# Loading q and k of five early tiles in 2-KB pieces and turning them with 64-column products

## The chip, the cores and the metric

The kernel runs on one core of one Trainium2 chip. The metric is the device time of one execution in microseconds (us); of three timed runs of the kernel before, the median is 197.52 us (197.02 to 198.58). Engines are named as in the profile: PE is the matrix engine (PEld its weight loads), DVE the vector engine, ACT the scalar engine, POOL the engine whose queue issues the loads from memory, SP the engine whose queue issues the stores and the transposing DMAs.

## The reference

Two stages follow each other. The first is attention with 4 batches, 8 heads, 768 positions and head size 64. Position i sees the 8 first positions and the 96 last ones up to its own; the score carries a slope per head times the distance. The result, written as 3072 tokens of 512 numbers, goes through a two-layer network: `relu(x @ w_in) ** 2 @ w_out` with `w_in` 512 x 2048 and `w_out` 2048 x 512.

```python
scores = scale * np.matmul(q, k.transpose(0, 1, 3, 2))
scores = np.where(keep, scores + bias, -1e9)      # keep: first 8 keys, or 0 <= i - j < 96
a = np.exp(scores - scores.max(-1)); a = a / a.sum(-1)
x = np.matmul(a, v)                               # -> (3072, 512)
out = np.maximum(x @ w_in, 0.0) ** 2 @ w_out
```

## The kernel before, in words

The 3072 tokens are 24 tiles j of 128 positions (six per batch); two tiles make a block of 256 tokens for the network, so there are 12 blocks. For a tile the chain is: load q and k (type changed to bfloat16 on the way), turn them so that the head dimension lies on the partitions (`tr.0.j` for q, `tr.1.j` for k on PE into a PSUM bank, `T.0.j` and `T.1.j` copy the bank to `qkT` on ACT or DVE), bias products (`bias`, tiles 0 to 2 only), score products (`sc`), exponentials on ACT (`exp`), a multiplication by a mask on DVE (`mul`, from tile 3 on), the products with v (`pv`), a division on DVE (`norm`), turning the result (`trx` on PE and `xT` as its copy, tiles 0 to 7). `gk` and `gv` copy the 8 global keys and values from the batch's first tile into the next ones. From tile 8 on q and k are turned by transposing DMAs.

The network's first layer is `s1.block.step` in plain form (block 0 and half of block 1), and later `h.block.group.product` with seven products for eight (Strassen's scheme), with sums of the weights (`isum`, `wsum`), copies `u`, additions `c` and squares `q`. The second layer is `s2.block.product` with `part` copies, `o` results and `st` stores.

The order of all this is written out by hand in `ORDER` (line 57 on). It is a list of names; each engine runs its own names in the order of the list, one after the other, and waits in front of each one for whatever that needs. `@A` and `@V` put a copy on ACT or DVE, the hex digits behind a colon pick PSUM banks or buffers. So an engine never runs a later name while an earlier one waits. The SBUF pieces `qk_first` hold q and k of tiles 0 to 5; later the same memory takes `isum`.

Tile 0 comes through SP in float32 (`plain`). Tiles 1 to 5 are loaded by `load_part` on POOL: every row of 64 numbers of a head is one 256-byte piece, 1024 pieces for 128 positions and 8 heads. The issuing line in the profile is L330. `emit_tr` (L528) turns a tile with four 128x128 transposes, one for each pair of heads, and `emit_T` (L455 on DVE, L453 on ACT) copies the bank, which holds bfloat16. In `ORDER` fourteen loads stand before the first load of `w_in`, `ld.win.1.0`, on POOL's queue: the ten loads of q and k and those of v for tiles 0 to 3.

Of the kernel before, what the change touches and what calls it, by code (L numbers as in the profile page):

```python
# [62 lines left out]
trx.1:6 exp.3.0.1 exp.3.1.0:7 exp.3.0.0 ld.win.1.0 pv.2.0:2 pv.2.1:5 norm.2.0:0 norm.2.1 gv.2@V mul.3.0:8 sc.4.0:1037
exp.4.1.0:9 trx.2:2 ld.win.4.0 xT.1@A exp.4.1.1:a tr.1.5:4 tr.0.5:5 T.1.5@A exp.4.0.0 xT.2@A:1 mul.3.1:b pv.3.0:0
pv.3.1:6 T.0.5@A s1.0.1:7 norm.3.0:1 gk.4@V exp.4.0.1 norm.3.1 gv.3@A s1.0.1#2 trx.3:4 sc.5.0:0126 exp.5.0.1:c
exp.5.1.0:d s1.0.4:5 exp.5.1.1 E0.0 mul.4.0:e xT.3@V ld.v.4 mul.4.1:f ones.6 pv.4.0:3 s1.1.1:4 relu.0.4@V:2 exp.5.0.0
ld.win.3.0 s1.0.3:2 pv.4.1:1 relu.0.1@A:0 sq.0.1@A:0 gv.4@A s1.0.3#2 mul.5.1:1 s1.1.3:6 norm.4.0:0 norm.4.1 ld.win.2.0
ld.win.0.0 s1.0.0:5 relu.0.3@A:3 sq.0.3@A mul.5.0:5 gate.10 s1.0.2:0 trx.4:7 relu.1.1@A:4 sq.1.1@A:1 xs.1.0:0 ld.v.5
ld.win.2.1 pv.5.0:3 ld.win.0.1 pv.5.1:1 xs.1.1 ld.win.6.0 ld.win.7.0 ld.win.5.0 relu.1.3@A:7 norm.5.0:1 norm.5.1
ld.wout.3 s1.1.2:2 xT.4@A:2 relu.1.2@A:8 ld.wout.2 ld.wout.1 ld.wout.0 isum.0.0 s1.1.0:4 s1.0.2#2 trx.5:3 gate.14  # L70
xT.5@V relu.1.0@A:6 sq.1.2@A s1.0.0#2 xs.2.0:1 h.2.0.p1:1 sq.1.0@V sq.0.4@A u.2.0.1@A:b isum.3.0 sq.1.3@A xs.2.1
ld.wout.7 isum.0.1 s1.0.0#3 s1.0.6:6 gate.11 isum.1.0 isum.1.1 xs.1.2 s1.0.7:7 h.2.0.p2:2 c.2.0.c11:9 h.2.1.p1:3
relu.0.6@A:a ld.wout.6 ld.wout.5 ld.wout.4 u.2.1.1@A:e relu.0.7@A:c isum.3.1 s1.0.0#4 h.2.1.p5:4 s1.0.2#3 relu.0.0@A:f
h.1.1.p1:6 h.2.1.p2:7 u.1.1.1@A:0 isum.2.1 h.2.1.p6 u.2.1.2@A:d h.1.1.p2:2 c.1.1.c11:3 xs.2.2 c.2.1.c11:5 sq.0.0@A
s1.0.2#4 isum.2.0 h.1.1.p6 u.1.1.2@A:1 h.2.0.p6 u.2.0.2@A:4 h.2.1.p7 u.2.1.3@A:8 h.1.1.p7 h.2.0.p5:5 relu.0.2@A:6
u.1.1.3@A:2 h.2.0.p7 wsum.0.0 h.1.1.p5:2 u.2.0.3@A:7 c.2.1.c22:b wsum.1.0 sq.0.2@A gate.9 s1.0.5:7 h.2.1.p3 wsum.2.0
c.2.0.c22:f load.6 load.7 c.1.1.c22:0 sq.0.7@A relu.0.5@A:e sq.0.6@A sq.0.5@A load.8 c.2.1.c12:8 sum.0.2:0 sum.0.0
h.1.1.p4 h.2.0.p4 wsum.0.1 s2.1.p1.0:0 T.8 c.2.0.c21@A:6 h.2.0.p3 h.2.1.p4 s2.0.p1.0:7 h.1.1.p3 sum.0.1 s2.0.p2.0:4
q.1.1.c22@A q.1.1.c11@A s2.0.p1.1 q.2.1.c22@A:2 q.2.0.c11@A part.0.p1@A:0 c.1.1.c21@A:c s2.0.p2.1 s2.1.p1.1 wsum.1.1
s2.0.p6.0 s2.0.p6.1 c.1.1.c12:7 tr.1.6:1 tr.0.6:6 part.1.p1@A:1 q.1.1.c21@A s2.1.p2.0:2 q.2.1.c11@A sum.0.3 wsum.2.1  # L80
part.0.p6@A:2 o.0.p2:a c.2.1.c21@A:2 s2.1.p2.1 wsum.3.1 wsum.3.0 T.1.6@V s2.0.p7.0 s2.0.p7.1 gate.12 s2.0.p5.0
q.1.1.c12@A s2.0.p5.1 c.2.0.c12:e load.9 part.0.p7@A:3 q.2.1.c12@A T.0.6@A q.2.0.c22@A o.0.p5:d s2.0.p4.0 s2.0.p4.1
q.2.0.c12@A o.0.p4@A sum.1.0:1 s2.0.p3.0 tr.0.7:3 gate.13 sum.1.1 s2.0.p3.1 o.1.p2:0 o.0.p3 sum.1.2 T.0.7@A tr.1.7:1
sum.2.2:0 sum.1.3 sum.2.0 T.1.7@A q.2.0.c21@A s2.1.p6.0 s2.1.p6.1 q.2.1.c21@A part.1.p6@A:0 sc.6.0:567341 exp.6.1.0:3
load.10 gk.7@A exp.6.0.0 s2.1.p5.0 s2.1.p7.0 s2.1.p7.1 mul.6.0:b exp.7.0.0:9 exp.7.1.0 part.1.p7@A:3 s2.2.p1.0:6
s2.1.p5.1 sum.2.1 exp.7.0.1:1 exp.7.1.1 o.1.p5:c mul.7.0:5 s2.2.p1.1 pv.6.0:5 norm.6.0:0 s2.1.p4.0 s2.1.p4.1 o.1.p4@A
pv.6.1:7 s2.1.p3.0 sc.8.0:3415 exp.8.0.1:7 part.2.p1@A:1 pv.7.0:0 s2.1.p3.1 mul.7.1:8 norm.6.1 T.9 pv.7.1:7 norm.7.0:1
norm.7.1 trx.6:1 exp.8.1.0:4 xT.6@V:0 exp.8.1.1 exp.8.0.0 s2.2.p6.0 s2.2.p6.1 o.1.p3 gate.15 trx.7:0 xT.7@A gk.8@V
mul.8.1:f h.3.1.p1:4 u.3.1.1@A:e gv.7@V h.3.0.p2:7 sc.9.0:5132 exp.9.0.1:6 exp.9.1.0:2 xs.3.0:0 xs.3.1 exp.9.0.0
h.3.0.p1:0 h.3.1.p6 mul.8.0:3 s2.2.p2.0:3 u.3.0.1@V:9 pv.8.0:1 u.3.1.2@A:b T.10 c.3.0.c11:1 h.3.0.p6 pv.8.1:5  # L90
norm.8.0:0 exp.9.1.1 sum.2.3 norm.8.1 xs.3.2 part.2.p6@A:2 xT.8:2 s2.2.p2.1 h.3.1.p7 h.3.1.p5:7 u.3.0.2@A:5
u.3.1.3@A:8 c.3.1.c22:7 o.2.p2:4 mul.9.0:3 mul.9.1:9 h.3.0.p7 s2.2.p7.0 s2.2.p7.1 u.3.0.3@A:f q.3.1.c22@A:0
part.2.p7@A:3 q.3.0.c11@A h.3.0.p5:2 h.3.1.p2:1 c.3.1.c11:8 gv.8@V load.11 c.3.0.c22:7 h.3.1.p3 h.3.0.p4 c.3.0.c21@A:2
h.3.1.p4 c.3.1.c21@A:1 q.3.1.c11@A c.3.1.c12:6 s2.2.p5.0 pv.9.0:5 gk.9@V T.11 st.0.0 norm.9.0:1 q.3.1.c12@A
q.3.0.c22@A h.3.0.p3 pv.9.1:1 gv.9@A c.3.0.c12:e norm.9.1 s2.3.p1.0:0 s2.2.p5.1 sc.10.0:4752 exp.10.1.1:f h.4.0.p1:1
s2.2.p4.0 exp.10.1.0:3 s2.2.p4.1 q.3.0.c12@V s2.3.p1.1 sum.3.0:1 o.2.p5:b s2.2.p3.0 s2.2.p3.1 exp.10.0.1 exp.10.0.0
part.3.p1@A:0 sum.3.1 h.4.1.p1:2 s2.3.p6.0 o.2.p4@A mul.10.0:8 s2.3.p6.1 sum.3.2 pv.10.0:7 mul.10.1:9 o.2.p3 gk.10@A
xT.9 norm.10.0:0 xs.4.0:1 xs.4.1 h.4.1.p2:5 pv.10.1:4 q.3.1.c21@A q.3.0.c21@A part.3.p6@A:1 u.4.1.1@A:6 u.4.0.1@A:5
s2.3.p7.0 s2.3.p7.1 h.4.1.p6 u.4.1.2@A:7 norm.10.1 h.4.0.p6 u.4.0.2@A:e gate.18 sc.11.0:6374 exp.11.1.0:a exp.11.0.0
gv.10@V c.4.1.c11:3 part.3.p7@V:3 sum.3.3 xs.4.2 load.12 h.4.0.p2:5 T.12 exp.11.1.1:1 h.4.1.p7 s2.3.p4.0 mul.11.0:2  # L100
exp.11.0.1 c.4.0.c11:f u.4.1.3@A:8 mul.11.1:9 load.13 h.4.0.p7 h.4.1.p5:3 c.4.1.c22:6 s2.3.p2.0:6 pv.11.0:4
u.4.0.3@A:a norm.11.0:1 q.4.1.c11@A:1 h.4.1.p4 h.4.0.p5:7 c.4.0.c22:5 s2.3.p2.1 o.3.p2:2 pv.11.1:5 q.4.1.c22@A
h.4.1.p3 q.4.0.c11@A gate.16 norm.11.1 h.4.0.p4 c.4.1.c21@A:1 c.4.0.c21@A:3 h.4.0.p3 s2.3.p4.1 c.4.1.c12:8 q.4.1.c12@A
c.4.0.c12:6 T.13 s2.3.p5.0 s2.3.p5.1 o.3.p5:9 q.4.0.c22@A q.4.0.c21@A o.3.p4@A sc.12.0:425137 exp.12.0.0:a st.2.1
exp.12.1.0 exp.13.0.0:b exp.13.1.0 exp.13.0.1:f q.4.0.c12@V s2.3.p3.0 sum.4.2:0 sum.4.0 xT.10:1 h.5.1.p1:0 s2.3.p3.1
mul.12.0:7 s2.4.p1.0:4 xT.11 o.3.p3 gate.19 xs.5.0:0 xs.5.1 h.5.0.p1:2 u.5.0.1@A:e q.4.1.c21@A h.5.1.p2:5 s2.4.p1.1
sum.4.1 part.4.p1@A:2 u.5.1.1@A:8 load.15 load.14 st.2.0 st.3.1 h.5.0.p5:1 pv.12.0:6 h.5.0.p6 mul.13.0:5 h.5.0.p2:3
c.5.0.c11:3 norm.12.0:0 s2.4.p6.0 xs.5.2 u.5.0.2@A:6 exp.13.1.1 mul.13.1:a q.5.0.c11@A:2 h.5.1.p6 h.5.0.p7 pv.12.1:7
u.5.0.3@A:4 s2.4.p2.0:3 s2.4.p6.1 s2.4.p2.1 pv.13.0:6 c.5.0.c22:1 gk.13@V h.5.0.p3 u.5.1.2@A:9 c.5.1.c11:b h.5.0.p4
norm.13.0:1 q.5.0.c22@A part.4.p6@A:0 norm.12.1 pv.13.1:5 norm.13.1 o.4.p2:e h.5.1.p7 gate.21 c.5.0.c12:3 h.5.1.p5:6  # L110
s2.4.p7.0 s2.4.p7.1 c.5.0.c21@A:7 q.5.0.c21@A u.5.1.3@A:f load.16 st.1.0 T.14 q.5.1.c11@V c.5.1.c22:0 h.5.1.p4 T.15
sum.4.3 T.16 sc.14.0:7251 xT.12:0 gv.13@A xT.13 q.5.1.c22@V q.5.0.c12@A s2.4.p5.0 part.4.p7@A:3 gate.17 exp.14.1.0:4
# [1337 lines left out]
```

## Time and profile before

| | |
|---|---|
| Median of three runs | 197.52 us |
| The profiled execution | 197.45 us, its span 195.7 us |
| PE busy | 188.5 us, 96% of the span |
| DVE busy | 179.4 us, 92% |
| ACT busy | 161.6 us, 83% |
| POOL busy | 75.1 us, 38% |
| First product of the network (`s1.0.1`) | 19.66 us after the start of the span |
| Last product | 8 products from 191.36 us on |

A product on PE is counted as busy from its start until its result is out, about 0.22 us for 128 columns, while the next one starts after 0.056 us. A busy PE therefore does not mean a stream without gaps: this is read from the starts of the products. Durations on DVE and ACT can be taken as they are.

### The profile page before, as it was taken

The page shows a single profiled execution, that of the slowest core. Times are in us where ns is not written, and L with a number is a line of the kernel's source. Part 1 is how long each engine was busy: PE and PEld are TensorE (multiplying, and loading weights), DVE is VectorE, ACT ScalarE, POOL GpSimd, SP SyncE. Part 2 cuts the span into 40 slices and gives each one's busy share as a digit, 9 for nine tenths or more (in the row PEclk, how much of TensorE's full clock was granted, in tenths as well). Part 3 has the DMA queues.
Part 4 walks back from the last instruction along what each step waited for, and adds up shares of the span by engine and source line. Part 5 has one row for each costly group of instructions (what it writes and reads, how often), then busy time and mean ns, then how long its engine had stood idle before and what let it go on. Part 6 is the DMA issues. An engine that isn't in the chain of part 4 may idle for free.

```text
span 195.7 us, 6835 instructions
## 1 busy us (share of the span) xinstructions
PE 188.5 (96%) x2808; PEld 170.5 (87%) x2808; DVE 179.4 (92%) x437; ACT 161.6 (83%) x338; POOL 75.1 (38%) x93
## 2 busy tenths in 40 slices
PE   7986999999999999999999999999999999999993
PEld 3774999999888989989989989989889999999982
DVE  8569989999999999989999999899999899999982
ACT  6699999999989797999899997587987798986600
POOL 8999784775564502650047080119200000000000
...
GB/s 125 149 150 167 179 193 205 205 162 151 155 150 143 99 177 168 119 100 227 139 79 129 138 74 119 209 168 97 147 113 188 85 136 13 20 193 105 0 91 234
DMA packets 111713, 26.92 MB, mean 138 GB/s; under 512 B 103234, under 2 KB 108866, under 8 KB 111682
## 3 DMA queue, kind: packets, MB, share of 16 engines
...
q8 instruction: 22, 0.36, 0.7%
q14 instruction: 9, 0.07, 0.1%
...
## 4 chain that ended last, share of the span: by engine, by line
PE 85%; POOL 6%; DMA 5%; DVE 1%; issue 0%; POOLq 0%; DVEq 0%
PE bank L1230 37%; PE bank L967 32%; PE bank L1081 6%; PE bank L618 5%; PE bank L767 5%; POOL qk_first L330 5%; DMA win<-in_moe_w_in_dram 3%; DMA xT<-x 2%; POOL v L330 2%; PE bank L835 1%; PE bank L528 0%; DVE xs L939 0%; DVE buf L886 0%; DVE hsum L1185 0%; DVE early L1305 0%
## 5 line engine op out<-in xcount | busy, mean ns | idle before, releaser
L684 ACT ACTIVATE buf<-bank 128x512 bf16<-128x512 f32 x76 | 41.5, 613 | 2.8 <-PE bank L618 2.7
L1031 ACT ACTIVATE hs<-buf 128x512 bf16<-128x512 f32 x62 | 37.2, 635 | 2.5 <-DVE buf L1011 2.0
L1230 PEld LDWEIGHTS <-hsum 128*128 128x128 bf16 x384 | 35.3, 98 | 4.0
L453 ACT COPY buf<-bank 128x512 f32<-128x512 f32 (+1 forms) x59 | 32.1, 569 | 7.7 <-PE bank L967 6.1
L1230 PE MATMUL bank<-wsum,hsum 128*128 128x256 bf16 x288 | 38.0, 273 | 0.0
L1011 DVE CUSTOM_DVE_ANT_0 buf<-bank,buf 128x512 f32<-128x512 f32 x49 | 33.0, 682 | 0.8 <-ACT buf L453 0.3
L967 PEld LDWEIGHTS <-qk_first 128*128 128x128 bf16 x504 | 31.1, 98 | 1.4 <-issue 0.3
L967 PEld LDWEIGHTS <-win 128*128 128x128 bf16 x504 | 30.8, 98 | 0.9
L334 POOL DMA_DIRECT2D qk<-in_q_dram x18 | 16.0, 889 | 35.3 <-DMA qkT<-qk 30.0
L1230 PEld LDWEIGHTS <-hs 128*128 128x128 bf16 x288 | 26.3, 98 | 2.7
L1230 PE MATMUL bank<-wout,hs 128*128 128x256 bf16 x192 | 27.3, 273 | 0.0
L334 POOL DMA_DIRECT2D v<-in_v_dram x18 | 16.0, 891 | 23.1 <-PE bank L967 13.1
L967 PE MATMUL bank<-xs,qk_first 128*128 128x128 bf16 x336 | 24.6, 219 | 0.2 <-DVE buf L886 0.2
L967 PE MATMUL bank<-xT,win 128*128 128x128 bf16 x336 | 24.6, 219 | 0.0
L709 DVE TENSOR_TENSOR buf<-buf,E 128x1024 bf16<-128x1024 bf16 x32 | 21.5, 683 | 0.5 <-ACT buf L684 0.5
L798 DVE TENSOR_TENSOR x<-bank,rs 128x256 bf16<-128x256 f32 x48 | 20.4, 425 | 1.7
L767 PE MATMUL bank<-v,buf 128*128 128x65 bf16 x312 | 16.1, 193 | 0.9 <-DMA v<-in_v_dram 0.5
L1185 DVE TENSOR_TENSOR hsum<-hs 128x1024 bf16<-128x1024 bf16 (+1 forms) x26 | 16.4, 642 | 0.3
L334 POOL DMA_DIRECT2D qk<-in_k_dram x18 | 16.1, 897 | 0.6 <-DMA wout<-in_moe_w_out_dram 0.4
L767 PEld LDWEIGHTS <-buf 128*128 128x128 bf16 x312 | 13.9, 98 | 1.8 <-DVE buf L709 0.6
L884 ACT ACTIVATE buf<-bank 128x512 f32<-128x512 f32 x23 | 13.7, 607 | 1.0 <-PE bank L967 1.0
L453 ACT COPY part<-bank 128x256 f32<-128x256 f32 x29 | 11.1, 383 | 3.6 <-PE bank L1230 3.6
...
## 6 DMA issues: line engine op xcount, KB each, us to landing
...
```

What stands on the lines that cost most here:

```text
L334: nc.gpsimd.dma_start(out=dst, in_=src)
L453: nc.scalar.copy(dst, src)
L684: nc.scalar.activation(out=tiles[tag, j, g][:, odd], in_=tiles.pop(("sc", j, odd, g)).rearrange("p a c -> p (a c)"), func=Act.Exp, scale=s ...
L709: nc.vector.tensor_mul(at, tiles.pop(("esc", j, g)), bias)
L767: nc.tensor.matmul(out=po[:, hi, :], lhsT=tiles["at", j, g][:, odd, at * P : (at + 1) * P], rhs=v_sb[kj][:, h, :], start=(i == 0), stop=(i ...
L798: nc.vector.tensor_tensor(out=x[:, 4 * hf : 4 * hf + 4, :], in0=po[:, :, :D], in1=rs.to_broadcast([P, 4, D]), op=Alu.mult,)
L884: nc.scalar.activation(dst, src, Act.Relu)
L967: nc.tensor.matmul(out=tiles["h", blk, g, bank][:, n], lhsT=left_[:, s, k], rhs=right_[:, k], start=opens and n == 0 and k == 0, stop=k == ...
L1011: nc.vector._custom_dve(TENSOR_ADD_SAT, out=hr, in0=src, in1=tiles.pop(("u", blk, g, i)), s0=float("inf"), s1=0.0,)
L1031: nc.scalar.activation(hs, hr, Act.Square)
L1185: nc.vector.tensor_tensor(out=t[:, i, h], in0=t[:, a, h] if isinstance(a, int) else half_a(blk, *a)[:, h], in1=t[:, b, h] if isinstance(b, ...
L1230: nc.tensor.matmul(out=tiles["acc", blk, bank][:, cols], lhsT=left_[:, s], rhs=right_[:, cols], start=first and s == 0, stop=s == NSTEP - ...
```

## The change

For tiles 1 to 5, q and k are loaded in another layout: one partition holds eight consecutive positions of one head, which lie together in memory as 2 KB, so one load has 128 pieces in place of 1024. What was 128 positions by 512 numbers is now (8 heads x 16 groups) by (8 rows x 64 numbers). The turning is then done by 16 products for each load: for every row r of the eight and each parity of the heads, the 128x64 piece of that row is the weight, and 64 columns of the identity (the four heads of this parity) are streamed through, into partitions 0 to 63 or 64 to 127 of a bank of float32. The copy that takes the bank to `qkT` also puts the positions in order: it writes in steps of eight positions, 16 bytes apart. The products with v name the load of the previous tile's v as a dependency too. `ORDER` is a new list with the same 1230 names; 10 of the 16 `T` copies stand on ACT where it was 6.

```diff
 ORDER = """
-tr.0.0:0 T.0.0@V tr.1.0:1 bias.0.0:23 T.1.0@V ld.q.1 ld.k.1 tr.0.1:4 T.0.1@V ld.q.2 ld.k.2 E0.1 ld.q.3 ld.v.0 ld.k.3
-tr.1.1:5 T.1.1@A ld.v.1 sc.0.0 bias.1.0:6701 exp.0.1.0:0 sc.1.0 tr.0.2:4 exp.0.0.0 gk.1@A T.0.2@V exp.1.0.0:1 tr.1.2:5
...
+tr.0.0:0 tr.1.0:1 bias.0.0:23 ld.q.1 ld.k.1 tr.0.1:4 tr.1.1:5 T.1.1@V ld.q.2 ld.k.3 ld.q.3 T.0.0@A ones.6 T.1.0@A
+sc.0.0 ld.k.2 tr.0.2:6 T.0.1@A bias.1.0:7014 sc.1.0 E0.1 exp.0.0.0:0 exp.0.1.0 T.0.2@V gk.1@A exp.1.1.1:1 ld.v.0
+tr.0.3:5 T.0.3@V gate.9 exp.1.1.0:3 tr.1.3:2 tr.1.2:3 bias.2.0:6450 exp.1.0.1 ld.v.1 ld.k.4 pv.0.0:1 T.1.2@V sc.2.0
+T.1.3@A exp.1.0.0 exp.2.1.1:4 pv.0.1:3 pv.1.0:2 tr.1.4:7 exp.2.0.0:5 exp.2.1.0 ld.q.5 norm.0.0:0 ld.k.5 ld.q.4 ld.v.2
+ld.win.1.0 gk.2@V norm.0.1 exp.2.0.1 sc.3.0:1036 exp.3.1.1:6 trx.0:4 norm.1.0:1 T.1.4@V pv.1.1:2 xT.0@V:0 exp.3.0.1
+exp.3.1.0:7 gv.1@V gk.3@V ld.v.3 tr.1.5:7 tr.0.4:5 pv.2.0:6 norm.1.1 trx.1:4 T.0.4@V pv.2.1:3 exp.3.0.0 xT.1@A T.1.5@A
+norm.2.0:0 sc.4.0:2015 tr.0.5:6 T.0.5@A gv.2@V mul.3.1:8 mul.3.0:9 s1.0.1:4 pv.3.1:7 pv.3.0:6 exp.4.1.1:a ld.win.3.0
+s1.0.1#2 norm.2.1 trx.2:3 ld.win.4.0 exp.4.0.0:b exp.4.1.0 norm.3.0:1 norm.3.1 gk.4@A exp.4.0.1 s1.0.3:5 s1.0.3#2
+trx.3:2 ld.v.4 mul.4.0:c mul.4.1:d xT.2@A:1 ld.win.2.1 xT.3@V ld.win.0.1 relu.0.3@A:e sc.5.0:6071 relu.0.1@A:f
...
     def load_part(n, j):
+        if j < NFIRST + 2:
+            swdge(
+                ("qk"[n], j), qk_all[:, j, n], src_rows((q, k)[n], j).rearrange("h (g r) d -> h g (r d)", r=8), 0.70,
+            )
+            return
         swdge(
...
             def emit_tr(e, j=j, n=n, fp=fp):
                 tr = psum(0, FP32 if fp else BF16).rearrange("p (a c) -> p a c", a=NPAIR)
+                if 1 <= j < NFIRST + 2:
+                    tr = psum().rearrange("p (r a g) -> p r a g", r=8, a=NPAIR)
+                    src = qk_all[:, j, n].rearrange("p (r d) -> p r d", d=D)
+                    for r in range(8):
+                        for odd in range(2):
+                            nc.tensor.matmul(
+                                out=tr[odd * D : (odd + 1) * D, r], lhsT=src[:, r],
+                                rhs=ident.rearrange("p (a o g) -> p o a g", a=NPAIR, o=2)[:, odd],
+                                start=r == 0, stop=True, skip_group_check=True,
+                            )
+                    tiles["tr", n, j] = tr
+                    return
...
             def emit_T(e, j=j, n=n, T_=T_):
-                any_copy(e, T_[:, n], tiles.pop(("tr", n, j)))
+                tr = tiles.pop(("tr", n, j))
+                if 1 <= j < NFIRST + 2:
+                    any_copy(
+                        e, T_[:, n].rearrange("p a (g r) -> p r a g", r=8), tr
+                    )
+                    return
+                any_copy(e, T_[:, n], tr)
...
             if not first:
-                deps.append(glob.get(("v", j - 1)))
+                deps += [land["v", j - 1], glob.get(("v", j - 1))]
```

More of the change, by code (lines that the diff above doesn't have):

```diff
@@ L63 @@
[L63 to L112, printed above, removed]
@@ new lines @@
+q.2.1.c22@A sum.1.0:1 part.1.p1@A:3 sum.1.1 s2.0.p3.0 o.1.p2:b s2.0.p4.1 s2.0.p3.1 s2.1.p6.0 s2.1.p6.1 T.0.7@A
+q.2.0.c12@A o.0.p4@A T.1.7@A sum.1.2 o.0.p3 part.1.p6@V:0 load.8 T.8 sum.1.3 q.2.1.c11@A q.2.1.c12@A q.2.1.c21@A
+s2.1.p5.0 sc.6.0:314702 s2.1.p7.0 sum.2.0:0 sum.2.1 exp.6.1.0:1 exp.6.0.0 exp.7.0.1:c s2.1.p7.1 s2.1.p5.1 s2.2.p1.0:1
+load.9 s2.2.p1.1 mul.6.0:0 part.1.p7@A:2 gk.7@V pv.6.0:3 exp.7.1.0:7 pv.6.1:0 s2.1.p4.0 s2.1.p4.1 load.10
+part.2.p1@A:3 exp.7.0.0 exp.7.1.1 o.1.p5:2 o.1.p4@A q.2.0.c21@A s2.1.p3.0 norm.6.0:0 mul.7.0:8 T.9 st.0.0 norm.6.1
@@ new lines @@
+sc.8.0:7342 gk.8@A exp.8.1.0:3 exp.8.1.1:e pv.7.0:6 trx.6:0 mul.7.1:a s2.2.p6.0 pv.7.1:3 xT.6@A:0 s2.1.p3.1 s2.2.p6.1
+norm.7.0:1 exp.8.0.1 exp.8.0.0 norm.7.1 gv.7@V sum.2.3 o.1.p3 trx.7:6 xT.7@A xs.3.0:0 xs.3.1 h.3.0.p1:2 h.3.1.p1:0
+u.3.0.1@A:d u.3.1.1@A:4 h.3.0.p2:3 sc.9.0:4756 part.2.p6@A:1 exp.9.0.1:f exp.9.1.1 exp.9.1.0:1 T.10 sum.2.2 mul.8.0:0
+load.11 T.11 mul.8.1:7 xs.3.2 h.3.0.p6 h.3.1.p6 u.3.1.2@A:9 c.3.0.c11:8 load.12 s2.2.p2.0:5 s2.2.p2.1 pv.8.0:6
+u.3.0.2@A:5 pv.8.1:7 h.3.1.p7 norm.8.0:0 gate.13 o.2.p2:c norm.8.1 h.3.1.p2:3 load.13 gv.8@A s2.2.p7.0 h.3.1.p5:6
@@ L169 @@
+s2.11.p4.0 s2.11.p4.1 o.11.p4@A:3 st.11.1#2 o.11.p5 st.11.1 sum.11.3#2 s2.11.p3.0 s2.11.p3.1 o.11.p3 st.11.0#2
 """
```

151 lines of the change are left out of this document (92 added, 59 removed).

## The prediction

> **What bounds the kernel now.** I read the page's shares first, then the chain that ended last, then the windows of the first 26 us.
>
> ```profile
> span 195.7 us, 6835 instructions
> PE 188.5 (96%) x2808; PEld 170.5 (87%) x2808; DVE 179.4 (92%) x437; ACT 161.6 (83%) x338; POOL 75.1 (38%) x93
> PE 85%; POOL 6%; DMA 5%; DVE 1%; issue 0%; POOLq 0%; DVEq 0%
> ```
>
> Three engines are above 80%, so a cost on any of them can count. The chain says where it is not PE: 11% lie on POOL and DMA. In order of time:
>
> ```profile
> 1.35 4.52 POOL qk_first L330 x5
> ...
> 12.86 0.74 POOL v L330
> 13.60 6.01 DMA win<-in_moe_w_in_dram
> 19.66 1.07 PE bank L1081 x16
> ...
> 33.39 1.79 PE bank L967 x32
> ...
> 182.77 9.64 PE bank L1230 x88
> ```
>
> Fourteen loads are issued one after the other (1.35 to 13.60 us), then the first piece of w_in takes 6.01 us to land, and only then, at 19.66 us, does the network begin. From there PE is the chain: 32 products of 128 columns in 1.79 us are 0.056 us each, 88 of 256 columns in 9.64 us are 0.110 each, without a gap worth the name. So the kernel has two parts: a front of 19.66 us with holes on PE, and a stream of about 172.7 us (19.66 to 192.4) in which PE is full. The stream can only get longer; a gain has to come out of the front.
>
> ```profile
> 8.00:10.00 2.00, 2.00 (x34) 1.61 (x33) 0.51 (x2) 1.71 (x6) 2.00 (x3) 1.00 2.42 154
> 10.00:12.00 2.00, 2.00 (x39) 1.54 (x37) 0.59 (x3) 2.00 (x7) 2.00 (x4) 1.00 2.39 152
> 12.00:14.00 2.00, 1.41 (x40) 1.23 (x39) 1.86 (x8) 2.00 (x5) 2.00 (x3) 1.00 2.26 150
> 14.00:16.00 2.00, 1.24 (x24) 0.89 (x21) 1.97 (x6) 1.96 (x5) 2.00 (x4) 1.00 2.36 147
> 16.00:18.00 2.00, 1.74 (x42) 1.40 (x38) 1.84 (x7) 1.87 (x5) 2.00 (x4) 1.00 1.68 161
> 18.00:20.00 2.00, 1.35 (x26) 0.96 (x24) 1.95 (x6) 2.00 (x5) 2.00 (x4) 1.00 1.68 186
> ```
>
> Columns after the window: its length, then PE, PEld, DVE, ACT, POOL busy. ACT is full from 8 us on, DVE from 12 us on, with some 3 us free between 8 and 12. Only POOL's queue is full throughout. The front is thus close to balanced: what is taken from the loads meets ACT and DVE at once.
>
> How much PE has free there follows from rates:
>
> ```profile
> 4.58 1.54 PE L528 MATMUL bank<-ident,plain 128*128 128x128 f32 x8
> 17.52 0.49 PEld L528 LDWEIGHTS <-qk_first 128*128 128x128 bf16 x8
> 18.37 0.31 PEld L767 LDWEIGHTS <-buf 128*128 128x128 bf16 x8 [0.36 <-DVE buf L709]
> 20.51 0.27 PEld L835 LDWEIGHTS <-x 128*128 128x128 bf16 x4
> 20.88 0.45 PEld L618 LDWEIGHTS <-qkT 64*128 64x128 bf16 x16
> 21.43 0.77 PEld L1081 LDWEIGHTS <-win 128*128 128x128 bf16 x8
> ```
>
> A weight load of the last product of a group ends some 0.05 us after its start, so a full 128-column product costs 0.056, a product with 65 columns (L767) about 0.031, one of 64 rows (L618) 0.028. Between 4.58 and 19.66 us PE streams 8 float32 transposes (1.3 us), 24 bias products (2.2), 40 transposes (40 x 0.056 = 2.2), 72 scores (2.0), 56 with v (1.7) and 12 `trx` (0.7): 10.1 of 15.1 us. **Five us are free**, and this is all that can be won.
>
> **The change part by part.**
>
> ```profile
> L330 POOL DMA_DIRECT2D qk_first<-in_q_dram x5 | 4.8, 958 | 0.2 <-issue 0.2
> 5.81 0.93 POOL L330 DMA_DIRECT2D v<-in_v_dram  x1
> 6.68 0.94 POOL L330 DMA_DIRECT2D qk_first<-in_k_dram  x1
> 15.96 2.38 POOL L330 DMA_DIRECT2D win<-in_moe_w_in_dram  x3
> 25.17 2.82 POOL L330 DMA_DIRECT2D wout<-in_moe_w_out_dram  x4 [0.29 <-DMA win<-in_moe_w_in_dram]
> ```
>
> (1) *Loads.* A load of 1024 pieces holds POOL's queue for 6.68 - 5.81 = 0.87 us. One of 512 pieces (w_in) takes about 0.75, one of 256 (w_out) 0.70. A load of 128 pieces does not occur; above it is bounded by 0.87, below by 0.66 (the last halving saved 0.05). I take 0.70, the nearest row. In the new list ten loads of q and k and three of v stand before `ld.win.1.0`: 1.35 + 10 x 0.70 + 3 x 0.87 = 10.96 us in place of 13.60; with the same 6.01 us it lands at 17.0, 2.7 us earlier. With 0.87 it would be 18.7, which still decides nothing, as step 4 shows.
>
> (2) *Products.* 160 products with 64 columns replace 40 transposes. No row has a 128x64 weight. Bounds: 0.028 (L618) and 0.056 (L528); I take 0.031, since 65 columns are the nearest length. Sum 160 x 0.031 - 2.2 = **+2.7 us** on PE (+2.2 to +6.7), about 0.5 us for each load where it was 0.22. Every step between products of 64 rows and of 128 costs more: after the 16 L618 loads end at 21.33, the next begins at 21.43, 0.1 us. If 64-column weights do the same, six runs of them make up to 12 such steps, some of which exist already: +0.5 (0 to 1.2).
>
> [...]
>
> (3) *Copies.*
>
> ```profile
> L455 DVE COPY qkT<-bank 128x512 bf16<-128x512 bf16 x8 | 3.1, 418 | 2.9 <-PE bank L528 2.9
> 5.68 1.29 DVE L455 CAST qkT<-bank 128x512 bf16<-128x512 f32 x2 [0.59 <-PE bank L528]
> L453 ACT COPY qkT<-bank 128x512 bf16<-128x512 bf16 x6 | 3.5, 604 | 1.6 <-PE bank L528 1.6
> L453 ACT COPY buf<-bank 128x512 f32<-128x512 f32 x51 | 29.3, 600 | 6.2 <-PE bank L967 6.1
> 7.48 0.59 ACT L453 COPY qkT<-bank 128x512 bf16<-128x512 bf16 x1 [1.59 <-PE bank L528]
> ```
>
> On ACT float32 costs what bfloat16 does (0.60). On DVE it is 0.645 against 0.418: six copies there, +0.23 each, but two float32 ones leave for ACT, so DVE's sum hardly moves and ACT takes four copies more. Two of these run where ACT had 1.6 us idle (the wait of its first `qkT` copy for L528). Writing 16 bytes apart is in no row: from nothing to half again a copy (+0.3); I take nothing, the float32 rows being the nearest, and keep the other end as rival B. Three `gv` and a square move to DVE as well (0.4 and 0.7 us), up to +1.8 us by the time all three engines are full.
>
> (4) *The order in the front.*
>
> ```profile
> 11.49 2.58 ACT L684 ACTIVATE buf<-bank 128x512 bf16<-128x512 f32 x5
> L798 DVE TENSOR_TENSOR x<-bank,rs 128x256 bf16<-128x256 f32 x48 | 20.4, 425 | 1.7
> L797 DVE RECIPROCAL rs<-bank 128x4 f32<-128x4 f32 x48 | 8.7, 180 | 0.6
> L709 DVE TENSOR_TENSOR buf<-buf,E 128x1024 bf16<-128x1024 bf16 x32 | 21.5, 683 | 0.5 <-ACT buf L684 0.5
> 8.68 0.45 PEld L618 LDWEIGHTS <-qkT 64*128 64x128 bf16 x16 [0.21 <-ACT early L684]
> 10.66 0.45 PEld L618 LDWEIGHTS <-qkT 64*128 64x128 bf16 x16 [0.21 <-DVE qkT L455]
> 12.66 0.45 PEld L618 LDWEIGHTS <-qkT 64*128 64x128 bf16 x16 [0.76 <-DVE qkT L455]
> 16.34 0.45 PEld L618 LDWEIGHTS <-qkT 64*128 64x128 bf16 x16
> ```
>
> The last four are the scores of tiles 1 to 4 before. I follow the new list by hand, each name starting when its engine is free and what it needs is there, with an exponential at 2.58 / 5 = 0.52, a division at 0.18 + 0.425 = 0.6 and a mask at 0.68 us. PE now has no hole early: `tr` of tile 1 ends at 7.4 us, `sc.1` at 9.7 (it was 9.1), three more loads turned to 11.2, `bias.2` 12.1, `sc.2` 12.8 (11.1 before), `tr.1.4` 13.8, `sc.3` 14.6 (13.1 before; waits for `norm.0.1` on DVE), `sc.4` 18.1 (16.8 before; waits for T.0.4 behind `norm.1.1`). Attention is some 1.5 us *later* than before, for PE itself is what it waits for until 14 us, then DVE. `s1.0.1` comes at 18.7 to 19.1, against 19.66. The weights, there at 17.0 (or 18.7), no longer hold it. At that point `pv.3` (16 x 0.031) and `trx.2` (0.22) are not yet done, together 0.72 us, which were done before 19.66 in the kernel before. Start -0.8, undone work +0.7: nothing won.
>
> (5) *Behind it.* `pv.3.0` waits 0.4 us for `mul.3.0`, `pv.4` 0.2 for `gv.3`, `pv.5.0` 0.45 for `mul.5.0`: +1.0. PE's queue waits with each, since it takes its names in order. The steps of (2) that the walk has only in part: +0.4. Sum **+1.4 us**.
>
> (6) *The rest.* The second dependency of `pv` is met already: `pv` of the tile before waited for that load on the same queue. From 40 us on the same 1230 names run in another order. As PE was full there, this can win at most 0.5 us and lose 1.5; I take nothing, the mean row being a full PE. The last store's path after the last product is the same.
>
> So 197.45 (the profiled execution; span 195.7 and 1.75 around it) + 1.4 = **198.9 us**. The profiled execution lies 0.07 below the median of three.
>
> **The rivals.**
>
> A. *Slow products.* Each of the 160 costs 0.056 like a full one. Against my 0.031 that is 4.0 us, and at least seven of the ten groups lie before 14 us where PE is the bound: +2.8 to +4.0, so 201.7 to 202.9. For it speaks that the weight has still 128 rows; against it that 64-row weights (L618) go at 0.028. It decides once PE has no hole left in the front. This one ends clearly slower.
>
> B. *Slow copies.* Six DVE copies ahead of `s1.0.1` at 0.95 instead of 0.645 us are +1.8, two thirds of it on the path (DVE is the bound from 14 us): 200.1. [...]
>
> C. *Faster.* Two products of one row go to the two halves of PE and overlap, so that a load costs the old 0.22 us. Then PE has its holes back, DVE and ACT run from 7 us on, and the earlier weights count: `s1.0.1` at about 17.5, less the 0.7 undone, less part of the stalls of (5): 1 to 2 us below before, 195.5 to 196.5. In its favour: pairs of L618 do overlap (two in 0.056). Against it: ACT was full from 8 us on and now has more to do.
>
> D. *The loads are not shorter* (0.87 each). The weights land at 18.7 and k, q of tile 4 up to 1.5 us later: 199.0 to 199.5, little apart from the forecast.
>
> **How the numbers follow.** Forecast with D 0.47, own range 197.3 to 200.0; A 0.20; B 0.13; C 0.15; a rest of 0.05 for a late stall in the new order (above 200). About 1% is what a measurement of this kernel can tell from no change: 195.5 to 199.5. Faster: half of C and a little, 0.12. Slower: A, most of B, a fifth of the forecast, the rest: 0.43. Same: 0.45. The range leaves the lower edge of C and the upper one of A out: 195.9 to 202.3.
>
> **What would show it.** The `qk_first` issues at 0.66 to 0.75 us each; the first w_in issue near 11 us. Groups of 16 weight loads (128x64) in 0.45 to 0.55 us: 0.85 would be A, 0.25 C. DVE copies of 128x512 from float32 at 0.65: 0.95 is B. `s1.0.1` at 18.7 to 19.1 us, with no wait for w_in in front of it. Scores of tile 4 near 18 us. From 30 us on PE full, the last product near 193.8. I am wrong if `s1.0.1` starts near 17.5, if attention is not later than before, or if PE shows new gaps after 40 us of over 1.5 us in all.

## The result, and the profile after

| | before | after |
|---|---|---|
| Median, five runs each | 197.58 us (197.02 to 199.51) | 213.83 us (211.71 to 216.24) |
| The profiled execution, its span | 197.45 us, 195.7 us | 211.71 us, 209.9 us |
| First product of the network | 19.66 us | 28.21 us |
| Last group of products begins | 191.36 us | 205.57 us |

The ratio is 1.0775, with a 95% interval of 1.0725 to 1.0826: clearly slower. The run of 216.24 us lies over 1.5% above the fastest of its five, and the verdict goes by the other four. The forecast was 198.9 us and its range ended at 202.3 us.

From the page of the kernel after, the shares, the granted TensorE clock by slices of 5.2 us, and the engines of the chain that ended last:

```profile
span 209.9 us, 7107 instructions
PE 196.0 (93%) x2928; PEld 177.0 (84%) x2928; DVE 188.6 (90%) x433; ACT 171.1 (81%) x342; POOL 72.7 (35%) x93
...
PEclk9996557999999999999999999999999999999999
...
PE 60%; DMA 10%; SPq 2%; ACT 1%; issue 1%; DVE 1%; POOL 0%; POOLq 0%; DVEq 0%; ACTq 0%
```

All three busy engines gained busy time: PE 7.5 us, DVE 9.2, ACT 9.5. And there is something that the profile of before did not have at all: a stretch of the span in which TensorE ran at half its clock. The instructions on the tile `qkT` say where most of DVE's and ACT's gain is from; the new order also moves other work between the two (columns: line, engine, operation, tile, count, then shortest, median and longest in ns, first and last start):

```profile
L458 ACT CAST qkT<-bank x6: 587/2438/2445, 5.7 to 28.3; 128x512 bf16<-128x512 f32 x6
L460 DVE CAST qkT<-bank x6: 2422/2438/2660, 7.9 to 24.2; 128x512 bf16<-128x512 f32 x6
```

The two copies of tile 0 on ACT, which write side by side, still take 0.59 us. Each of the ten that write 16 bytes apart takes **2.44 us**, on either engine. Six of them on DVE are 6 x (2.44 - 0.69) = 10.5 us more there, four on ACT are 4 x (2.44 - 0.59) = 7.4 us more, and all of it lies before 31 us. The timeline and the waits of PE's queue show what that does:

```profile
11.00 6.97 DVE L460 CAST qkT<-bank 128x512 bf16<-128x512 f32 x3
...
13.47 0.60 PE L620 MATMUL bank<-pb,early 128*128 128x256 bf16 x4 [1.41 <-DVE qkT L460]
...
15.74 0.60 PE L620 MATMUL bank<-pb,early 128*128 128x256 bf16 x4 [1.67 <-DVE v L507]
...
18.02 0.29 PE L641 MATMUL bank<-qkT 64*128 64x128 bf16 x2 [1.57 <-DVE rs L820]
...
28.21 1.03 PE L1104 MATMUL bank<-xT,win 128*128 128x128 bf16 x8
```

```profile
PE bank L641 <- DVE rs L820: 2.7, 2, 1.6
PE bank L620 <- DVE v L507: 1.7, 1, 1.7
PE bank L620 <- DVE qkT L460: 1.4, 1, 1.4
...
PE bank L790 <- ACT qkT L458: 1.1, 1, 1.1
PE bank L620 <- ACT qkT L458: 0.9, 1, 0.9
PE bank L536 <- DVE qkT L460: 0.7, 1, 0.7
```

(The first number is the sum in us, then how often, then the longest.) Three copies in a row hold DVE for 7 us. PE waits for them, or for a small step queued behind them: the reciprocal L820 and a memset L507. These six lines are 8.5 us of standing still; before, one wait of 0.6 us for a `qkT` copy was the longest of this kind. The windows show the second half of the damage (columns: length, then PE, PEld, DVE, ACT, POOL busy, granted clock):

```profile
10.00:15.00 5.00, 2.52 (x71) 1.96 (x71) 4.97 (x9) 4.78 (x9) 5.00 (x6) 1.00 1.62 182
15.00:20.00 5.00, 2.69 (x44) 2.23 (x45) 4.10 (x9) 1.54 (x4) 4.63 (x7) 0.71 1.77 180
20.00:25.00 5.00, 4.32 (x91) 3.96 (x86) 4.91 (x10) 3.24 (x7) 4.18 (x7) 0.50 1.84 180
25.00:30.00 5.00, 3.52 (x57) 3.08 (x56) 4.13 (x8) 4.61 (x3) 2.36 (x4) 0.50 1.36 200
30.00:35.00 5.00, 4.19 (x56) 4.06 (x55) 2.69 (x8) 3.90 (x9) 3.84 (x5) 0.58 1.24 206
```

From 10 to 20 us PE was busy for half of the time. In finer windows the granted clock falls to 0.50 at about 17.2 us, and it is back at 1.00 only at about 34.2 us.

So of the 14.2 us between the two spans 8.55 lie ahead of the network (28.21 against 19.66) and 5.7 behind its start (177.4 us from first to last product against 171.7).

### The profile page after: what moved, and what is told of

Same layout as the page of the kernel before. It is cut to its first block, busy times and chain, and to the rows that moved or that the text cites. A ratio compares the mean times of both kernels' runs of the same rounds, so it can differ in the third digit from the quotient of the medians.

```text
span 209.9 us, 7107 instructions
## 1 busy us (share of the span) xinstructions
PE 196.0 (93%) x2928; PEld 177.0 (84%) x2928; DVE 188.6 (90%) x433; ACT 171.1 (81%) x342; POOL 72.7 (35%) x93
## 4 chain that ended last, share of the span: by engine, by line
PE 60%; DMA 10%; SPq 2%; ACT 1%; issue 1%; DVE 1%; POOL 0%; POOLq 0%; DVEq 0%; ACTq 0%
PE bank L1253 28%; PE bank L990 24%; PE bank L641 3%; PE bank L790 3%; DMA out_dram<-buf 3%; DMA qkT<-qk 3%; DMA xT<-x 2%; DMA qk<-in_k_dram 2%; SPq L577 1%; ACT hs L1054 1%; PE bank L545 0%; PE bank L1104 0%; DVE buf L1328 0%; SPq L882 0%; DVE xs L962 0%
## 5 line engine op out<-in xcount | busy, mean ns | idle before, releaser
L458 ACT COPY buf<-bank 128x512 f32<-128x512 f32 (+1 forms) x58 | 31.3, 565 | 10.1 <-PE bank L1253 4.9
L1253 PE MATMUL bank<-wsum,hsum 128*128 128x256 bf16 x288 | 38.6, 273 | 0.0
L707 ACT ACTIVATE buf<-bank 128x512 bf16<-128x512 f32 x56 | 32.4, 628 | 6.1 <-PE bank L641 4.5
L1054 ACT ACTIVATE hs<-buf 128x512 bf16<-128x512 f32 x57 | 34.8, 643 | 0.1
L1034 DVE CUSTOM_DVE_ANT_0 buf<-bank,buf 128x512 f32<-128x512 f32 x46 | 30.9, 686 | 0.8 <-ACT buf L458 0.2
L1253 PE MATMUL bank<-wout,hs 128*128 128x256 bf16 x192 | 26.5, 273 | 0.0
L707 ACT ACTIVATE early<-bank 128x512 bf16<-128x512 f32 x32 | 18.5, 620 | 0.2
L460 DVE CAST qkT<-bank 128x512 bf16<-128x512 f32 x6 | 14.3, 2507 | 3.3 <-PE bank L536 3.3
L641 PE MATMUL bank<-qkT 64*128 64x128 bf16 x192 | 13.4, 229 | 2.7 <-DVE rs L820 2.7
L641 PEld LDWEIGHTS <-qkT 64*128 64x128 bf16 x352 | 10.9, 100 | 5.9 <-issue 3.0
```

The lines of the kernel that those rows point to most:

```text
L458: nc.scalar.copy(dst, src)
L460: nc.vector.tensor_copy(dst, src)
L641: nc.tensor.matmul(out=tiles["sc", j, odd, g][:, at, :], lhsT=left[j - 1][half, pair, :] if kt else qkT[j % NKT][half, 1, pair, :], rhs=qk ...
L707: nc.scalar.activation(out=tiles[tag, j, g][:, odd], in_=tiles.pop(("sc", j, odd, g)).rearrange("p a c -> p (a c)"), func=Act.Exp, scale=s ...
L1034: nc.vector._custom_dve(TENSOR_ADD_SAT, out=hr, in0=src, in1=tiles.pop(("u", blk, g, i)), s0=float("inf"), s1=0.0,)
L1054: nc.scalar.activation(hs, hr, Act.Square)
```

## The experiments

Three theories of where the time comes from were put up. S: the copies that write 16 bytes apart. O: the new order of the list. P: the loads and the 64-column products.

**The copies write side by side.** The changed kernel, but the ten copies leave the bank's order as it is (positions and heads inside a tile are then mixed, so the scores belong to other pairs; the work is the same).

```diff
-                        e, T_[:, n].rearrange("p a (g r) -> p r a g", r=8), tr
+                        e, T_[:, n].rearrange("p a c -> p (a c)"), tr.rearrange("p r a g -> p (r a g)")
```

> The changed kernel, but the copies of tiles 1 to 5 write their bank one number after the other; the positions of q and k are left out of order, so the scores are those of other pairs. Theory S (spread writes): the copies cost 0.6 us in place of 2.44, PE has no long holes, the granted clock stays at 1.0 and the time is 196.5 to 199.5 us, where the prediction stood. Theory O (the new order is late by itself): the copies get short but the time stays above 206 us. Theory P (loads and small products): the first product of w_in stays later than 25 us and the time above 206 us.

Measured: 200.03 us, ratio 1.0188 (1.0122 to 1.0254). The groups of copies, and the first and last products in the timeline:

```profile
L460 DVE CAST qkT<-bank 128x512 bf16<-128x512 f32 x6 | 4.0, 683 | 3.6 <-PE bank L536 3.6
L458 ACT CAST qkT<-bank 128x512 bf16<-128x512 f32 x6 | 3.5, 589 | 1.1 <-PE bank L545 0.6 <-PE bank L536 0.5
```

```profile
17.84 0.62 PE L1104 MATMUL bank<-xT,win 128*128 128x128 bf16 x8
...
192.91 1.04 PE L1253 MATMUL bank<-wout,hsum 128*128 128x256 bf16 x8
```

With copies of 0.59 and 0.68 us the network begins at 17.84 us, 1.8 us *earlier* than in the kernel before; the end is nevertheless later. The copies and the clock (1.00) came as theory S had them, but the time is a little above its 196.5 to 199.5 us. How much is left to explain is not sharp: three of the four runs (199.06 to 200.15 us) lie 0.9 to 1.5% above the median before, 197.19 us, and only the interval of the recorded ratio reaches down to that.

**The same order of positions, but the strides on the reading side.** The copy reads the bank 64 numbers apart and writes side by side; the result is that of the changed kernel.

```diff
-                        e, T_[:, n].rearrange("p a (g r) -> p r a g", r=8), tr
+                        e, T_[:, n].rearrange("p a (g r) -> p a g r", r=8), tr.rearrange("p r a g -> p a g r")
```

> The changed kernel, but the copies put the positions in order on the reading side: they read the bank 64 numbers apart and write one number after the other. Theory S: it is the writing side that costs, so copies of 0.60 to 0.70 us and 196.5 to 199.5 us. Its rival (any order that jumps costs, on whichever side): copies near 2.4 us and 211 to 216 us.

Measured: 201.1 us, ratio 1.0188 (1.0133 to 1.0244); the copies take 683 ns on DVE and 593 on ACT, as in the run above:

```profile
L460 DVE CAST qkT<-bank 128x512 bf16<-128x512 f32 x6 | 4.0, 683 | 6.8 <-PE bank L536 6.8
L458 ACT CAST qkT<-bank 128x512 bf16<-128x512 f32 x6 | 3.6, 593 | 2.8 <-PE bank L545 2.3 <-PE bank L536 0.4
```

Reading a bank with strides cost nothing here (683 ns in both runs on DVE, 593 against 589 on ACT); writing 16 bytes apart costs 1.8 us a copy (2.44 against 0.59 to 0.68). Against the changed kernel that is 1.0775 - 1.0188 = 5.9%, 11.6 us. The time is again above the range of theory S. The profiled execution, 201.66 us, is the longest of the four, and its network begins at 20.72 us, 2.9 us later than in the run above. The ten copies are not the reason, for PE is late ahead of them:

```profile
7.61 0.66 PE L545 MATMUL bank<-ident,plain 128*128 128x128 f32 x4 [1.97 <-DMA plain<-in_k_dram]
```

PE waited 1.97 us for k of tile 0, which took 6.3 us to land where it was 4.1 in the run above, and from about 9.0 to 12.4 us the granted clock was 0.50 (an estimate from its 0.90 and 0.76 in the windows of 5 to 10 and 10 to 15 us).

**Only the spread writing.** The kernel before, with its old loads, transposes and order; the copies of tiles 1 to 5 write 16 bytes apart (positions and heads inside a tile are thereby mixed).

```diff
+                if 1 <= j < NFIRST + 2:
+                    any_copy(
+                        e, T_[:, n].rearrange("p a (g r) -> p r a g", r=8),
+                        tr.rearrange("p a c -> p (a c)").rearrange("p (r a g) -> p r a g", r=8, a=NPAIR),
+                    )
+                    return
```

> The kernel before with its loads, transposes and order, but the copies of tiles 1 to 5 write 16 bytes apart; the positions of q and k are put out of order by it. Theory S: each of the ten copies takes 2.44 us in place of 0.4 to 0.6, PE gets holes before 30 us, the granted clock falls there, and the time is 208 to 216 us. Theories O and P: the copies are slower but the time stays under 203 us, since order and products are those of before.

Measured: 215.48 us, ratio 1.0933 (1.0895 to 1.097). One edit by itself does more harm than the whole change. From the page of this run (granted clock) and from the waits of its PE queue:

```profile
PEclk9995666699999999999999999999999999999999
```

```profile
PE bank L625 <- DVE rs L804: 8.0, 2, 4.2
PE bank L625 <- ACT qkT L453: 3.6, 2, 2.4
```

The banks hold bfloat16 here, and the copies take 2.44 us all the same, so the source's type is not what they pay for. The old order has seven of the ten copies on DVE, hence waits of up to 4.2 us, and the clock falls as in the changed kernel.

**Only the new order.** The kernel before with the new list: old loads, transposes and copies, and the old dependencies.

```diff
 ORDER = """
-tr.0.0:0 T.0.0@V tr.1.0:1 bias.0.0:23 T.1.0@V ld.q.1 ld.k.1 tr.0.1:4 T.0.1@V ld.q.2 ld.k.2 E0.1 ld.q.3 ld.v.0 ld.k.3
...
+tr.0.0:0 tr.1.0:1 bias.0.0:23 ld.q.1 ld.k.1 tr.0.1:4 tr.1.1:5 T.1.1@V ld.q.2 ld.k.3 ld.q.3 T.0.0@A ones.6 T.1.0@A
...
```

> The kernel before (256-byte loads, four transposes, plain copies) in the new order. Theory S: the order by itself costs little: 196.5 to 200 us, clock 1.0. Theory O: above 206 us.

Measured: 200.31 us, ratio 1.0167 (1.0109 to 1.0226). So the order, with the old loads under it, costs about 3.3 us; this is just above the 200 us that theory S allowed. The profiled execution, 201.72 us, is the longest of the four: in it PE waited 0.78 us for a load of q and 1.16 us for one of v between 15 and 18 us, and the granted clock was 0.50 from about 17.7 to 21.1 us (an estimate from its 0.77 and 0.89 in the windows of 15 to 20 and 20 to 25 us), where S had put it at 1.0.

**Everything but the new order and the spread writing.** The 2-KB loads, the 64-column products and the strided reading in the old list: the changed kernel with the copy edit of the second experiment and the `ORDER` of the kernel before.

> The changed kernel's 2-KB loads and 64-column products of tiles 1 to 5, with copies that read the bank 64 numbers apart and write side by side (0.59 to 0.68 us each as in the run with the strided reading), in the order of the kernel before. Theory O (the new order by itself costs the 3 us that the runs without spread writing still lie above the kernel before; loads and products cost about nothing): 196.5 to 198.5 us against 197.2 to 197.6 before. Rival P (the loads and products cost the 3 us, and the order as much in its own run by accident): 199.5 to 201 us. If the loads' 0.10 to 0.25 us per issue on GpSimd reach the end, it comes out up to 1 us below before.

Measured: 199.75 us, ratio 1.0111 (1.0048 to 1.0173). This speaks against O in the form in which it was written down: the loads and products are not free, and the time lies where P put it. Yet neither theory has it all, for 1.7% (order alone) and 1.1% (loads and products alone) stand against 1.9% for both together. The three intervals overlap: that each costs something is shown, which costs more is not. The first and last products of the profiled executions separate them:

| | network begins | last group begins | between |
|---|---|---|---|
| before | 19.66 | 191.36 | 171.7 |
| old order, strided reading | 20.79 | 192.12 | 171.3 |
| new order only | 20.53 | 195.50 | 175.0 |
| new order, strided reading | 20.72 | 195.54 | 174.8 |
| new order, positions left | 17.84 | 192.91 | 175.1 |
| the changed kernel | 28.21 | 205.57 | 177.4 |

Each row is a single execution, and the starts of 20.53 and 20.72 us hold the late loads named above. Whatever the front does, the part behind it is 3.1 to 3.4 us longer in the three runs that have the new list and quick copies. Part of that is work left over from the front: the products with v (296 of them after the network's start before, 312 in the new list) and the `trx` (20 and 24) that the prediction had at 0.7 us.

```profile
19.66:196.00 176.34, 15.08 (x296) 13.23 (x296) 1.00 1.20 136
```

```profile
17.84:198.00 180.16, 15.28 (x312) 13.06 (x312) 1.00 1.20 133
```

(Windows for the products with v alone, PE and PEld: the kernel before, and the new order with positions left.) The other 2.4 to 2.7 us come out by subtraction. The profiles name 1.4 to 2.0 us of waits of PE behind the network's start, against 0.5 before; the remainder is not accounted for. The longest waits do not stand in one place: the run with the new order alone has one of 0.65 us at 116 us for a transposing DMA, that with strided reading one of 0.97 us at 148 us for a result copy on DVE, that with positions left one of 1.38 us at 20 us for which the profile names no releaser. With the old order the loss lies ahead of the network (20.79 against 19.66):

```profile
L460 DVE CAST qkT<-bank 128x512 bf16<-128x512 f32 x9 | 5.9, 687 | 4.3 <-PE bank L545 1.5 <-ACT buf L707 1.4 <-PE bank L536 1.4
```

```profile
PE bank L641 <- DVE qkT L460: 1.3, 2, 0.9
```

The float32 bank makes a copy on DVE 0.69 us instead of 0.42; these nine are 5.9 us, where before they were about 4.0 (3.1 for eight and 1.3 for two, less one of 0.42 that isn't among them), and PE's wait for them grew from 0.6 to 1.3 us. This is not the whole of the 1.13 us. Some 0.6 us are there ahead of these copies: the bias products of tile 0 begin at 6.57 us, before at 5.96, since k of tile 0, the float32 load through SP, took 4.4 us to land in place of 3.9. In the six profiles with 2-KB loads this load took 4.1 to 6.3 us, in the three with 256-byte loads 3.9 to 4.0. That the quicker issues on POOL delay it was not tried.

**The holes filled.** The changed kernel, with 33 products of zeros in front of `bias.2`, `sc.2`, `sc.3` and `sc.4`, where PE stood still; they add nothing to the result.

```diff
+    FILL = {2: 8, 3: 3, 4: 8}
...
+        def fill(bank, n, opens=False):
+            for _ in range(n):
+                nc.tensor.matmul(
+                    out=bank.rearrange("p a c -> p (a c)"), lhsT=fillz[:, :P], rhs=fillz,
+                    start=opens, stop=opens, skip_group_check=True,
+                )
...
+            if j == 2:
+                fill(tiles["sc", j, 1, 0], 6, True)
...
+                if j == 2 and g == 1 and (0, 1) not in opened:
+                    fill(tiles["sc", j, 1, 0], 8)
...
+            if j in FILL:
+                fill(tiles["sc", j, 1, 0], FILL[j], j >= NBIAS)
```

> The changed kernel with products of zeros (512 columns, 33 in all) in those places of TensorE's queue where it stood still for 1.2 to 1.7 us ahead of bias.2, sc.2, sc.3 and sc.4; nothing else differs and the output is the same. If the granted clock falls because TensorE stands still (theory S with the clock as its second half): clock about 1.0 in the stretch from 15 to 35 us instead of 0.50 to 0.71, and 4 to 7 us less than the changed kernel: 207 to 210 us. If the clock falls for another reason, or if its fall costs nothing since the slow copies set the pace: within 1.5 us of the changed kernel, or longer by part of the 33 products (about 0.25 us each).

Measured: 208.51 us, ratio 1.0514 (1.0441 to 1.0587), against 1.0775 for the changed kernel: 2.6%, or 5.2 us less, with more work. By the two intervals the gain lies between about 1.7 and 3.5%. The two profiled spans differ by only 2.5 us (207.4 against 209.9); in the filled one k of tile 0 landed 1.1 us later, and PE waited 1.23 us for it. The windows:

```profile
15.00:20.00 5.00, 5.00 (x67) 2.91 (x66) 4.54 (x9) 1.85 (x4) 3.88 (x6) 1.00 1.77 181
20.00:25.00 5.00, 3.86 (x86) 2.78 (x86) 4.93 (x10) 3.92 (x9) 3.15 (x5) 1.00 1.84 179
25.00:30.00 5.00, 3.32 (x58) 2.18 (x56) 3.92 (x8) 4.88 (x3) 3.52 (x5) 1.00 1.37 201
```

The clock is 1.00 in every window up to 40 us, where it was 0.71 and 0.50. So the clock fell because PE stood still, and its fall was worth about 5 of the 11.6 us that the spread writing costs. What remains is put down to the waits themselves: the network begins at 27.32 us here, still 7.7 us later than before.

**As long, but not spread.** The version with strided reading, each of the ten copies done over (four times on ACT, three and a half times on DVE).

```diff
+                    out, in_ = T_[:, n].rearrange("p a (g r) -> p a g r", r=8), tr.rearrange("p r a g -> p a g r")
+                    for _ in range(3):
+                        any_copy(e, out, in_)
+                    if e == "ACT":
+                        any_copy(e, out, in_)
+                    else:
+                        any_copy(e, out[:, :2], in_[:, :2])
```

> The version with the strided reading and side-by-side writing in the new order, but each of the ten copies of tiles 1 to 5 is done over: four times on ScalarE, three and a half times on VectorE, so that it lasts about 2.35 to 2.4 us without writing one number apart from its neighbours. Theory S in its plain form (the spread copies cost what they last, and nothing else of spread writing matters): the changed kernel's time again, 211 to 215 us, with the granted clock down to about 0.5 to 0.7 between 15 and 35 us. If spread writing also slows other work while it runs (transfers, other engines' access to the memory): well below, 203 to 209 us.

Measured: 214.23 us, ratio 1.0836 (1.0759 to 1.0913), with the first network product at 29.89 us and the clock down as in the changed kernel:

```profile
15.00:20.00 5.00, 1.64 (x20) 1.21 (x19) 4.76 (x11) 0.99 (x2) 4.52 (x7) 0.72 1.73 180
20.00:25.00 5.00, 4.17 (x87) 3.59 (x83) 4.09 (x12) 4.13 (x8) 4.19 (x7) 0.60 1.89 176
```

The intervals of 1.0836 and 1.0775 overlap. Spread writing hurts by how long the copies hold their engines, and no further cost of it to others has to be assumed.

**What a copy costs by its steps.** Two kernels that only copy a 128x512 bank, four times each way on each engine. In the first, VectorE's lines are L60 (written side by side), L62, L64, L66 and L68 (lone bfloat16 numbers 4, 8, 16 and 32 bytes apart), L70 (strides in reading), L72 (from the state buffer, 16 bytes apart) and L74 (float32, 16 bytes apart); L76 to L90 are the same on ScalarE. Three of these lines:

```python
nc.vector.tensor_copy(dve_step1[i], bank)
nc.vector.tensor_copy(dve_step8[i].rearrange("p (c r) -> p r c", r=8), bank.rearrange("p (r c) -> p r c", r=8))
nc.vector.tensor_copy(dve_readstep[i].rearrange("p (c r) -> p c r", r=8), bank.rearrange("p (r c) -> p c r", r=8))
```

> Only copies, four of each kind on VectorE and on ScalarE, of one 128 x 512 float32 bank; the output is zeros and the reference's work is left out. Written bf16 side by side: 0.59 to 0.68 us. Written 16 bytes apart (eight numbers): 2.44 us on both. Open is where the price starts. If it is paid for each small piece that is written: bf16 written 4, 8, 16 and 32 bytes apart all take 2.4 us, as does float32 written 16 bytes apart and a copy whose source lies in the state buffer. If it is paid for each 16-byte stretch of memory that is touched again: 4 bytes apart about 1.2, 8 bytes about 1.8, 16 and 32 bytes 2.4 us. Reading 64 numbers apart and writing side by side: 0.59 to 0.68 us.

The groups of this run (busy us of four copies, then the mean ns of one, which overlaps the start of the next):

```profile
L82 ACT CAST act_step<-bank 128x512 bf16<-128x512 f32 x4 | 9.4, 2813 | 0.0
...
L66 DVE CAST dve_step<-bank 128x512 bf16<-128x512 f32 x4 | 9.2, 2580 | 0.0
...
L68 DVE CAST dve_step<-bank 128x512 bf16<-128x512 f32 x4 | 8.9, 2482 | 0.0
L80 ACT CAST act_step<-bank 128x512 bf16<-128x512 f32 x4 | 4.8, 1475 | 0.0
L72 DVE CAST dve_sbufstep<-zero 128x512 bf16<-128x512 f32 x4 | 4.7, 1453 | 0.0
L64 DVE CAST dve_step<-bank 128x512 bf16<-128x512 f32 x4 | 4.7, 1304 | 0.0
...
L74 DVE COPY dve_f32step<-bank 128x512 f32<-128x512 f32 x4 | 4.0, 1097 | 0.0
L70 DVE CAST dve_readstep<-bank 128x512 bf16<-128x512 f32 x4 | 2.6, 718 | 0.0
...
L62 DVE CAST dve_step<-bank 128x512 bf16<-128x512 f32 x4 | 2.5, 708 | 0.0
L60 DVE CAST dve_step<-bank 128x512 bf16<-128x512 f32 x4 | 2.5, 684 | 0.7 <-PE bank L36 0.7
```

On DVE nothing is paid at 4 bytes apart (on ACT four copies took 2.5 us, side by side 2.1); at 8 bytes it is 4.7 / 4 = 1.2 us a copy, at 16 bytes 2.3 us, and 32 bytes add nothing to that (8.9 / 4 = 2.2). So neither of the two guesses held: the price goes neither by the piece nor does it begin at 4 bytes. What fits these rows is a price for each 16-byte stretch that is entered: at 8 bytes apart 256 of them, at 16 bytes 512, by an estimate from the 1.2 and 2.3 us some 4.5 ns each (128 of them, at 4 bytes apart, would be 0.58 us and vanish in the 0.63 us that a copy takes anyway). Float32 at 16 bytes apart enters 512 as well, but takes only 1.0 us. Hence a second run, in which the numbers come in groups.

> Again only copies of a 128 x 512 float32 bank; the output is zeros and the reference's work is left out. Four of each kind on VectorE and on ScalarE. Known from the first such run, per copy: bf16 written 8 and 16 bytes apart 1.2 and 2.3 us, float32 written 16 bytes apart 1.0 to 1.1 us. Theory H (a lone number of 2 bytes costs its 16-byte stretch twice, a whole 4-byte word once): bf16 in pairs written 16 bytes apart 0.6 to 0.7 us, float32 written 8 bytes apart 0.6 to 0.7 us and 32 bytes apart 1.0 to 1.1 us, bf16 in groups of four or eight 0.6 to 0.7 us. Theory L (each 16-byte stretch touched costs the same for bf16, pairs or not): pairs 16 bytes apart 1.2 us, groups of four written 16 bytes apart 0.6 to 0.7 us. bf16 alone written 16 bytes apart again 2.3 to 2.4 us.

Its groups: L56 are bfloat16 pairs written 16 bytes apart, L58 groups of four, L62 float32 32 bytes apart, L66 lone bfloat16 numbers 16 bytes apart again, L68 the pairs on ScalarE (same columns):

```profile
L66 DVE CAST dve_half<-bank 128x512 bf16<-128x512 f32 x4 | 9.2, 2570 | 0.0
...
L62 DVE COPY dve_f32step<-bank 128x512 f32<-128x512 f32 x4 | 3.8, 1064 | 0.0
L56 DVE CAST dve_pair<-bank 128x512 bf16<-128x512 f32 x4 | 2.5, 683 | 0.7 <-PE bank L36 0.7
L58 DVE CAST dve_quad<-bank 128x512 bf16<-128x512 f32 x4 | 2.5, 678 | 0.0
...
L68 ACT CAST act_pair<-bank 128x512 bf16<-128x512 f32 x4 | 2.1, 619 | 0.0
```

Theory H held: two bfloat16 numbers side by side, 4 bytes, cost nothing extra (2.5 / 4 = 0.63 us a copy) at the same step of 16 bytes at which lone ones cost 2.3 us.

No version that was run beats the kernel before.

## Why the prediction was wrong, point by point

**(1) Loads: right in kind.** An issue was put at 0.70 us (0.66 to 0.87), and the first piece of w_in at 10.96 us. From the timeline of the kernel after:

```profile
2.73 0.60 POOL L330 DMA_DIRECT2D qk_first<-in_q_dram  x1
...
11.09 0.78 POOL L330 DMA_DIRECT2D win<-in_moe_w_in_dram  x1
```

0.60 us is below the lower bound, since the fall from 1024 to 512 and 256 pieces was carried on too timidly; the place of w_in came out within 0.13 us, as waits made up the difference: that was luck. Rival D is out. What the new loads might do to the load of tile 0 was not weighed; its k landed 0.2 us later here and up to 2.4 us later in the other runs with them.

**(2) Products: over-sized.** 0.031 us each was taken, and rival A feared 0.056. The weight loads of 16 and of 48 products, at full clock:

```profile
8.19 0.33 PEld L536 LDWEIGHTS <-qk_first 128*64 128x64 bf16 x16 [0.18 <-DMA qk_first<-in_q_dram]
...
11.11 0.84 PEld L536 LDWEIGHTS <-qk_first 128*64 128x64 bf16 x48
```

A single weight load of this kind takes 0.106 to 0.113 us there (0.096 to 0.099 for those of 128x128 in the trace of before), not the 0.05 that the prediction had. That is about (0.84 - 0.11) / 47 = 0.016 us each: 2.5 us for all 160 against 2.2 before, +0.3 instead of +2.7. Sixteen take 0.33 us, between the forecast's 0.45 and the 0.25 of rival C, so C's pace was nearly reached; that it comes from an overlap of two halves is not shown. In this trace the 64-column products, at 0.016 us each, follow one another faster than the score products with their 64 rows, at 0.028.

**(3) Copies: this step failed.** It took "writing 16 bytes apart" as nothing, "the float32 rows being the nearest", and bounded it by +0.3 us a copy. It measured +1.75 us on DVE and +1.85 on ACT, six times the upper bound. Slow copies stood in the text as rival B, at 0.95 us on DVE, and were there under-sized in the same way. No row of the trace bore on the step at all, and so half a copy was not a bound but a guess: all copies of that trace wrote side by side. The copy runs give the price on DVE: 2.3 us a copy with lone numbers 8 numbers apart, 1.2 us at 4 apart, and only at 2 apart the 0.63 us of side by side.

**(4) The walk through the front: right but for the copies and the clock.** It had the network begin at 18.7 to 19.1 us, and at 17.5 for rival C. With copies that write side by side, the same list begins it at 17.84 us, and at 20.72 in the profile with the late load of tile 0. With slow ones it is 28.21. In the first of these the scores of tiles 1, 2 and 4 begin at 9.30, 11.90 and 16.91 us; the walk's ends of 9.7, 12.8 and 18.1, less 0.45 for a group, mean 9.25, 12.35 and 17.65. So attention is later than before (8.68, 10.66, 16.34), as the walk said, and the walk was late by up to 0.9 us at the network's start, for which the products, priced too high, are the likely reason. That holes on PE would cost clock as well was nowhere in it: the granted clock was 1.00 in every quoted window of before, and it was carried over as a constant. The filled holes put this at about 5.2 us.

**(5) and (6), the order behind the front: under-sized.** Stalls of 1.0 us and undone work of 0.7 us were put down, and for the rest of the list "nothing", with 1.5 us as the worst. Measured is 3.1 to 3.4 us, of which 0.7 are the undone work as predicted; the other 2.4 to 2.7 us are only in part named as waits by the profiles. It is also why rival C fails although its early start is there in the run with positions left (17.84 us): the front's 1.8 us are lost again later. "PE was full there" only says that the *old* list kept PE full.

By the sum: +1.4 was forecast. The runs give about +3.7 us for the loads, products and order together (ratio 1.0188), and +11.6 us for the spread writing, some 5 of these by the clock.
